# Second layer of four row groups by one level of Strassen's algorithm, in a fused attention and MLP kernel

## The chip, the cores and the metric

The kernel runs on one core of a Trainium2 chip. The metric is the device time of one execution in microseconds (us). The engines are named as in the profile: PE (TensorE, matrix products), PEld (its weight loads), DVE (VectorE), ACT (ScalarE), POOL (GpSimd), SP (SyncE, which here issues the transfers).

A run counts as slow when it took over 1.5% more than the fastest run of the same kernel. Ratios and verdicts use fast runs alone. A ratio is the mean time of one kernel's fast runs over the mean of the other kernel's fast runs in the same rounds, so it is not quite the ratio of the medians that are quoted beside it.

## The reference

Nyström attention over 8 batches of 8 heads, 576 tokens, head size 64, and then a layer norm with a two-layer MLP (512 to 2048 to 512) and a residual. Only the second part is touched:

```python
def _moe_ref(x, g_ln, w_ch1, w_ch2):          # x: attention output, (8, 576, 512)
    mu = np.mean(x, axis=-1, keepdims=True)
    var = np.mean((x - mu) ** 2, axis=-1, keepdims=True)
    xn = (x - mu) / np.sqrt(var + 1e-06) * g_ln
    ch = np.maximum(xn @ w_ch1, 0.0) @ w_ch2
    return x + ch
```

## The kernel before

The 4608 rows are 36 blocks of 128, in 9 groups of 512 rows. Per group, the first layer gives hT (hidden by rows, fp16) and the second layer multiplies it by w2. Matrix work is fp16 with fp32 sums. Attention is computed for pairs of batches, and its instructions are woven into the MLP stream: `fill(n)` lets the stream go n turns (about one 512-column matmul each) between two attention steps. In the traces below an engine's instructions come in the order of the source (rsum, for one, starts on DVE at 194.88 us, behind the 16 weight mixes that were given to DVE before it), which is why the place of an instruction in the source matters.

```python
def center(j):                                 # rows are only centered ...
    ...
    pool.tensor_scalar(out=xn_of[j][:], in0=x_blk[j][:], scalar1=1.0, scalar2=negm,
                       op0=ALU.mult, op1=ALU.add)
...
psM = ctx.enter_context(tc.tile_pool(name="psM", bufs=3, space=PSUM))   # three PSUM tiles, tag "pm"
...
def mlp():
    for g in range(NGRP):
        ...                                    # group 0 differs; transposes of g come before
        for m in range(MCH):                   # first layer: 16 blocks of 128 hidden rows
            psh = psM.tile([P, 512], FP32, name="psh", tag="pm")
            for c in range(KCH):
                MM(psh[:], w1_16[:, c, ts(m, P)], xnT[:, c, :], start=..., stop=...)
                ...
            act(hT[:, m, :], psh[:], AF.Relu)
        for u in range(4):                     # second layer: 4 row blocks x 16 matmuls of 512
            pso = psM.tile([P, DM], FP32, name="pso", tag="pm")
            for m in range(MCH):
                MM(pso[:], hT[:, m, ts(u, P)], w2_16[:, m, :], start=..., stop=...)
                if u >= 2 and m % 8 == 3:
                    ...                        # transposes of the next group's rows
            # ... the deviation is applied to the sum here, with the residual
            dve.scalar_tensor_tensor(out=ot[:], in0=pso[:], scalar=rstds[g][:, u:u + 1],
                                     in1=x_blk.pop(j)[:], op0=ALU.mult, op1=ALU.add)
            store(j, ot)
...
counts += 2 * [[12, 12, 21, 21, 21, 17, 12, 12, 9, 8, 9, 8, 11] + 10 * [8]]
for c, after, count in zip(pairs, ...):        # the last pair: batches 6 and 7
    for step, _ in enumerate(attention2(c.bs, c)):
        fill(count[step])
        settle()
        ...
```

The softmax here doesn't subtract the row's maximum and nothing guards it: scores larger than these inputs give would overflow.

Of the kernel before, what the change touches and what calls it, by code (L numbers as in the profile page):

```python
# [9 lines left out]
FP16 = mybir.dt.float16  # L10
FP32 = mybir.dt.float32
UINT32 = mybir.dt.uint32
AF = mybir.ActivationFunctionType
ALU = mybir.AluOpType
AX = mybir.AxisListType

P = 128
# [3 lines left out]
def kernel(  # L21
# [534 lines left out]
    def attention2(bs, c):  # L556
# [118 lines left out]

        yield from rows_of(bs, ea, zcbd)

    ln_ready = {0}
    mvgs = {}
    xn_of = {}  # L680
# [8 lines left out]
    def block_done(j):  # L689
        g, u = divmod(j, 4)  # L690
        if u == 0:
            mvgs[g] = mstat.tile([P, 4, 2], FP32, name="mvg", tag="mvg")
        if g == 0:
            center_by_act(j)
            later.append(lambda: stats(j))
        elif g == 1:
            later.append(lambda: center_by_act(j))
        else:
            if by_act(j):
                later.append(lambda: stats_by_act(j))  # L700
            else:
                stats(j)
            later.append(lambda: center(j) if g <= mlp_at[0] + 1
                         else uncentered.setdefault(g, []).append(j))
        if u == 3:
            later.append(lambda: deviations(g))


    mlp_at, uncentered = [0], {}
# [4 lines left out]
    def settle():  # L714
        while later:
            later.pop(0)()
# [26 lines left out]
    def center(j):  # L743
        g, u = divmod(j, 4)
        negm = mvgs[g][:, u, 0:1]
        if not by_act(j):
            negm = mstat.tile([P, 1], FP32, name="negm", tag="negm")[:]
            pool.tensor_scalar(out=negm, in0=mvgs[g][:, u, 0:1], scalar1=-1.0, scalar2=0.0,
                               op0=ALU.mult, op1=ALU.add)
        xn_of[j] = mxn.tile([P, DM], FP16, name="xn", tag="xn")  # L750
        pool.tensor_scalar(out=xn_of[j][:], in0=x_blk[j][:], scalar1=1.0, scalar2=negm,
                           op0=ALU.mult, op1=ALU.add)

    def deviations(g):
        lnv = mstat.tile([P, 4], FP32, name="lnv", tag="lnv")
        for o in (0, 1):
            act(lnv[:, o::2], mvgs[g][:, o::2, 1], AF.Ln, bias=eps_ln[:],
                scale=1.0 / DM if by_act(4 * g + o) else 1.0)
        rstds[g] = mstat.tile([P, 4], FP32, name="rstd", tag="rstd")
        act(rstds[g][:], lnv[:], AF.Exp, scale=-0.5)  # L760
        ln_ready.add(g)
# [26 lines left out]
    def transposes(g):  # L788
        for u in range(4):
            transpose_block(g, u)  # L790
            yield



    def mlp():
        for g in range(NGRP):
            mlp_at[0] = g
            hT = mhT.tile([P, MCH, 512], FP16, name="hT", tag="hT")
            if g == 0:
                for u in (0, 2):  # L800
                    if u == 0:
                        for i in range(2):
                            transpose_block(0, i)
                            yield True
                    for m0 in range(0, MCH, 2):
                        if u == 0 and m0 in (6, 10):
                            transpose_block(0, 2 if m0 == 6 else 3)
                            yield True
                        if u == 0 and m0 < MCH - 6:
                            scale_w1(m0 // 2 + 3)  # L810
                        psh = psM.tile([P, 2, 256], FP32, name="psh", tag="pm")
                        for m in range(2):
                            for c in range(KCH):
                                MM(psh[:, m, :], w1_16[:, c, ts(m0 + m, P)],
                                   xnTs[0][:, c, ds(P * u, 256)],
                                   start=(c == 0), stop=(c == KCH - 1), skip=True)
                                if c == 1 or (c == 3 and m == 0):
                                    yield True
                        act(hT[:, m0:m0 + 2, ds(P * u, 256)], psh[:], AF.Relu)
                        yield True  # L820
            else:
                while g not in xnTs:
                    if g in ln_ready:
                        for _ in transposes(g):
                            yield True
                    else:
                        yield False
                xnT = xnTs.pop(g)
                for j in uncentered.pop(g + 1, ()):
                    center(j)  # L830
# [3 lines that stand above are left out]
                        MM(psh[:], w1_16[:, c, ts(m, P)], xnT[:, c, :],  # L834
                           start=(c == 0), stop=(c == KCH - 1))
                        if c < KCH - 1:
                            yield True
                    act(hT[:, m, :], psh[:], AF.Relu)
                    yield True
            tr = None  # L840
            for u in range(4):
                j = 4 * g + u
                pso = psM.tile([P, DM], FP32, name="pso", tag="pm")
                for m in range(MCH):
                    MM(pso[:], hT[:, m, ts(u, P)], w2_16[:, m, :],
                       start=(m == 0), stop=(m == MCH - 1))
                    if m < MCH - 1:
                        yield True
                    if u >= 2 and m % 8 == 3:
                        if g + 1 in ln_ready and g + 1 not in xnTs:  # L850
                            tr = transposes(g + 1)
                        if tr is not None:
                            next(tr, None)
                            yield True
                ot = mout.tile([P, DM], FP32, name="ot", tag="ot")
                dve.scalar_tensor_tensor(out=ot[:], in0=pso[:], scalar=rstds[g][:, u:u + 1],
                                         in1=x_blk.pop(j)[:], op0=ALU.mult, op1=ALU.add)
                store(j, ot)
                yield True
            if tr is not None:  # L860
                for _ in tr:
                    yield True
# [77 lines left out]
    for c, after, count in zip(pairs, pairs[1:] + [None], counts):  # L940
        for step, _ in enumerate(attention2(c.bs, c)):
            fill(count[step])
            settle()
            while c.jobs:
                c.next_job()
                c.next_job()
                fill(8)
            if after:
                cast_and_load(after, pairs[2])
                if step >= 1:  # L950
                    after.next_job()
# [32 lines left out]
```

## Time and profile before

| | before |
|---|---|
| time, median of the first 3 runs | 349.22 us (346.89 to 353.25, the last of them slow) |
| span of the profiled run | 346.7 us |
| PE, DVE, ACT, POOL busy | 93%, 46%, 49%, 36% |
| PE idle after 120 us | 0.3 us, and the end |

The prediction below shows the views that carry the argument. One more matters later. This is PE's timeline in the kernel before, around the end of group 6's second layer (columns: start, duration from the first start to the last end, engine, line, operation, output and inputs, shapes, how many; a wait stands in brackets):

```profile
282.73 0.39 PE L77 MATMUL psxt<-ident,xn 128*128 128x128 f16 x4
282.95 1.89 PE L73 MATMUL pso<-w,hT 128*128 128x512 f16 x8
284.68 0.39 PE L77 MATMUL psxt<-ident,xn 128*128 128x128 f16 x4
284.90 1.03 PE L73 MATMUL pso<-w,hT 128*128 128x512 f16 x4
285.77 1.46 PE L73 MATMUL psh<-xnT,w 128*128 128x512 f16 x6
```

Four matmuls stand between the last transposes and the next first layer (psh). They cover the time in which ACT copies the transposes to xnT, so psh starts without a wait.

### The profile page before, as it was taken

How to read it: one execution, taken by the hardware profiler on the slowest of the kernel's cores; microseconds unless marked ns; L12 is line 12 of the kernel's file. 1: busy time of each engine (PE TensorE's matmuls, PEld its weight loads, DVE VectorE, ACT ScalarE, POOL GpSimd, SP SyncE). 2: the span in 40 equal slices, each digit the busy share in tenths (PEclk: the TensorE clock that was granted, in tenths of full speed). 3: DMA queues.
4: the chain of work that ended last, by engine and by line, in shares of the span. 5: the costliest groups of instructions: out<-in, count | busy, mean ns of one | idle time of the engine just before them, and what ended most of it. 6: DMA issues, size and time to landing. Idle time of an engine off the chain costs nothing.

```text
span 346.7 us, 8948 instructions
## 1 busy us (share of the span) xinstructions
PE 323.3 (93%) x3818; PEld 166.4 (48%) x3818; DVE 158.7 (46%) x341; ACT 168.6 (49%) x328; POOL 125.5 (36%) x199
## 2 busy tenths in 40 slices
PE   8875979879889999999999999999999999999994
PEld 7553744435433545554445444544444454444441
DVE  2645629885499753346777402337850010020011
ACT  4359844943544595045738750465146226415600
POOL 2488878999953498047023000003120010000000
PEclk9999999989999999999999999999999999999998
DMA  7999999999982281171012101210130031022023
GB/s 274 357 353 362 344 404 369 233 384 317 236 281 91 62 260 47 32 201 32 2 30 64 31 2 42 55 30 2 34 84 6 15 77 32 0 62 61 0 54 69
DMA packets 21528, 46.72 MB, mean 135 GB/s; under 512 B 3056, under 2 KB 7152, under 8 KB 21488
## 3 DMA queue, kind: packets, MB, share of 16 engines
q1 hardware_dynamic: 21488, 46.15, 43.6%
q8 instruction: 30, 0.49, 0.6%
q14 instruction: 10, 0.08, 0.1%
HBM read 36.70 MB, written 9.44 MB: 133 GB/s over the span
## 4 chain that ended last, share of the span: by engine, by line
PE 75%; DVE 7%; DMA 7%; ACT 6%; issue 2%; SPq 1%; POOL 0%; DVEq 0%
PE psh L73 35%; PE pso L73 30%; DMA w1stg<-in_moe_w_ch_dram 4%; DMA g_sb<-in_moe_g_ln_dram 3%; PE pscv L73 3%; ACT xn L67 2%; PE psy L73 2%; PE psxt L77 2%; DVE st L67 2%; DVE xblk L67 2%; PE psn L73 1%; DVE xT L67 1%; ACT junk L67 1%; PE psea L73 1%; PE psec L73 1%
## 5 line engine op out<-in xcount | busy, mean ns | idle before, releaser
L73 PE MATMUL pso<-w,hT 128*128 128x512 f16 x576 | 137.6, 381 | 0.0
L73 PE MATMUL psh<-xnT,w 128*128 128x512 f16 (+1 forms) x640 | 133.7, 358 | 2.9 <-DVE xnT L67 1.2
L67 ACT ACTIVATE hT<-psh 128x512 f16<-128x512 f32 x144 | 85.3, 597 | 54.5 <-PE psh L73 54.3
L73 PEld LDWEIGHTS <-w 128*128 128x128 f16 x640 | 59.7, 98 | 60.6 <-issue 2.3
L73 PEld LDWEIGHTS <-hT 128*128 128x128 f16 x576 | 53.9, 98 | 55.7 <-issue 2.1
L67 DVE SCALAR_TENSOR_TENSOR ot<-pso,rstd,xblk 128x512 f32<-128x512 f32 x36 | 27.0, 749 | 107.7 <-PE pso L73 107.7
L67 ACT COPY xnT<-psxt 128x512 f16<-128x512 f16 x32 | 18.7, 584 | 59.1 <-PE psxt L77 59.0
L67 POOL CAST nat<-stg 128x1152 f16<-128x1152 f32 x28 | 31.8, 1147 | 5.1 <-DMA stg<-in_k_dram 1.8
L67 DVE TENSOR_TENSOR xblk<-psy,rcpd 128x512 f32<-128x512 f32 (+1 forms) x40 | 27.6, 691 | 1.8
L67 POOL TENSOR_SCALAR xn<-xblk,negm 128x512 f16<-128x512 f32 x18 | 12.5, 694 | 35.2 <-PE psxt L77 34.1
L67 DVE SCALAR_TENSOR_TENSOR st<-st,psn 128x384 f16<-128x384 f16 (+3 forms) x30 | 13.5, 450 | 24.2 <-PE psn L73 24.2
L67 POOL TENSOR_SCALAR xn<-xblk,mvg 128x512 f16<-128x512 f32 x10 | 6.9, 695 | 45.8 <-PE psxt L77 28.3
L67 POOL CAST natv<-stg 128x1152 f16<-128x1152 f32 x16 | 17.9, 1151 | 11.8 <-DMA stg<-in_v_dram 11.8
L67 DVE STREAM_TRANSPOSE xT<-nat 128x576 uint32<-128x576 uint32 x24 | 18.4, 767 | 4.8 <-POOL nat L67 3.5
L67 POOL TENSOR_SCALAR negm<-mvg 128x1 f32<-128x1 f32 x18 | 3.5, 192 | 37.6 <-PE psy L73 23.9
L73 PE MATMUL psy<-zcbd,ea 128*128 128x260 f16 (+1 forms) x80 | 16.0, 277 | 1.2 <-ACT xT L67 0.6
L77 PE MATMUL psxt<-ident,xn 128*128 128x128 f16 x144 | 14.2, 222 | 2.1 <-ACT xn L67 1.6
L67 DVE TENSOR_REDUCE lmk<-xT 128x64 f16<-128x1152 f16 x12 | 16.1, 1341 | 0.1
L67 POOL TENSOR_TENSOR asum<-asum 128x256 f32<-128x256 f32 (+2 forms) x30 | 15.0, 501 | 2.3
L67 DVE BATCH_NORM_STATS2 st<-xblk 128x6 f32<-128x512 f32 x22 | 15.2, 689 | 0.6
L77 PEld LDWEIGHTS <-xn 128*128 128x128 f16 x144 | 10.9, 99 | 9.1 <-ACT xn L67 2.0
L67 DVE RECIPROCAL rcpd<-psy 128x8 f32<-128x8 f32 (+1 forms) x40 | 8.0, 201 | 11.1 <-PE psy L73 10.6
(99 smaller groups left out, 257.6 us busy)
## 6 DMA issues: line engine op xcount, KB each, us to landing
stg<-in_q_dram SPq DMA_DIRECT2D x16, 576.0 KB, 6.9
stg<-in_k_dram SPq DMA_DIRECT2D x16, 576.0 KB, 7.8
out_dram<-ot SPq DMA_DIRECT2D x72, 128.0 KB, 2.4
stg<-in_v_dram SPq DMA_DIRECT2D x10, 576.0 KB, 8.2
w1stg<-in_moe_w_ch_dram SPq DMA_DIRECT2D x16, 256.0 KB, 6.0
w2stg<-in_moe_w_ch_dram SPq DMA_DIRECT2D x16, 256.0 KB, 5.2
stg<-in_v_dram SPq DMA_DIRECT2D x12, 288.0 KB, 8.7
g_sb<-in_moe_g_ln_dram SPq DMA_DIRECT2D x1, 2.0 KB, 10.1
```

The source lines that it names most:

```text
L67: return lambda *args, **kw: keep(getattr(self.engine, op)(*args, **kw))
L73: keep(nc.tensor.matmul(o, l, r, start=start, stop=stop, tile_position=(rb, cb), skip_group_check=(skip or cb != 0)))
L77: keep(nc.tensor.matmul(o, i_, idn, is_transpose=True, tile_position=(0, 0)))
```

## The change

For groups 4 to 7 the second layer becomes one level of Strassen's algorithm in Winograd's form. Rows and hidden are halved (h11 is the first half of the rows with the first half of the hidden, h12 has the second half of the hidden, h21 and h22 are the same for the second half of the rows), and so is w2. Seven products of half size take the place of eight, P1 to P7; the code calls their PSUM tiles psp1, psp4 and so on. The diff is cut; its comments were added here. The sums of h (here "mixes") are formed in place in hT by DVE between the products, those of w2 once. A group's rows are now fully normalized before the first layer, since the products mix rows. The outputs gather in the x tiles, and stores come from there.

```diff
+    def mix_w2():                              # 16 DVE instructions
+        ...
+        for i, a, b, op in ((1, w12, w11, ALU.subtract), (3, w22, w12, ALU.subtract),
+                            (2, None, w11, ALU.add), (4, w21, None, ALU.subtract)):
+            ...
+            for k in range(0, HK, 2):
+                dve.tensor_tensor(out=w2_mix[i][:, k:k + 2, :], in0=a[:, k:k + 2, :],
+                                  in1=b[:, k:k + 2, :], op=op)
+    def fast_second_layer(g, hT):
+        ...
+        def product(to, left, right, first=True):
+            for k_ in range(2):
+                for k in range(HK):            # 2 x 8 matmuls of 256 columns
+                    MM(to[:, k_, :], left[:, k, ts(k_, P)], right[:, k, :],
+                       start=first and k_ == k == 0, stop=k == HK - 1, skip=True)
+                    ...
+                if tr is None and g + 1 in ln_ready and g + 1 not in xnTs:
+                    tr = transposes(g + 1)
+                if tr is not None and not first:
+                    next(tr, None)             # only in the two products that accumulate
+                    yield True
+        def add(half, col, t):                 # two additions of 256 columns into x tiles
+            for i in range(2):
+                u = 2 * half + i
+                x = x_blk[4 * g + u][:, ts(col, HN)]
+                (pool if t is u2 else dve).tensor_tensor(out=x, in0=t[:, i, :], in1=x, op=ALU.add)
+        def mix(out, a, b, op):                # two instructions of 1024 fp16 elements
+            ...
+        pe = bank("psp4")
+        yield from product(pe, h22, w2_mix[4])                 # P4
+        add(1, 0, pe)
+        mix(h22, h21, h22, ALU.add)
+        pa = bank("psp1")
+        yield from product(pa, h11, w11)                       # P1
+        scalar.copy(p1, pa[:])
+        mix(h21, h11, h21, ALU.subtract)
+        pd = bank("psp7")
+        yield from product(pd, h21, w2_mix[3])                 # P7
+        add(1, 0, pd)
+        add(1, 1, pd)
+        mix(h11, h22, h11, ALU.subtract)
+        yield from product(pa, h12, w21, False)                # P2, onto P1
+        add(0, 0, pa)
+        pc = bank("psp5")
+        yield from product(pc, h22, w2_mix[1])                 # P5
+        add(1, 1, pc)
+        mix(h12, h12, h11, ALU.subtract)
+        pb = bank("psp6")
+        yield from product(pb, h11, w2_mix[2])                 # P6
+        dve.tensor_tensor(out=u2, in0=pb[:], in1=p1, op=ALU.add)
+        for half, col in ((1, 0), (1, 1), (0, 1)):
+            add(half, col, u2)                                 # six additions by POOL
+        yield from product(pc, h12, w22, False)                # P3, onto P5
+        add(0, 1, pc)
+        ...                                                    # four stores
@@ center: rows of groups 4 and up, after the group's deviations
+            pool.tensor_scalar(out=xn_of[j][:], in0=x_blk[j][:], scalar1=negm,
+                               scalar2=rstds[g][:, u:u + 1], op0=ALU.add, op1=ALU.mult)
@@ the loop of the last pair
             settle()
+            if c is pairs[2] and not w2_mix:
+                mix_w2()
```

More of the change, by code (lines that the diff above doesn't have):

```diff
@@ L676, in attention2 @@
         yield from rows_of(bs, ea, zcbd)
+    G_FAST = 4
     ln_ready = {0}
@@ L702, in block_done, with center_in_turn @@
                 stats(j)
-            later.append(lambda: center(j) if g <= mlp_at[0] + 1
-                         else uncentered.setdefault(g, []).append(j))
+            if g < G_FAST:
+                later.append(lambda: center_in_turn(j))
         if u == 3:
             later.append(lambda: deviations(g))
+            if g >= G_FAST:
+                for i in range(4 * g, 4 * g + 4):
+                    later.append(lambda i=i: center_in_turn(i))
+    def center_in_turn(j):
+        g = j // 4
+        if g <= mlp_at[0] + 1:
+            center(j)
+        else:
+            uncentered.setdefault(g, []).append(j)
     mlp_at, uncentered = [0], {}
@@ L750, in center @@
         xn_of[j] = mxn.tile([P, DM], FP16, name="xn", tag="xn")
-        pool.tensor_scalar(out=xn_of[j][:], in0=x_blk[j][:], scalar1=1.0, scalar2=negm,
-                           op0=ALU.mult, op1=ALU.add)
+        if g >= G_FAST:
+            pool.tensor_scalar(out=xn_of[j][:], in0=x_blk[j][:], scalar1=negm,
+                               scalar2=rstds[g][:, u:u + 1], op0=ALU.add, op1=ALU.mult)
+        else:
+            pool.tensor_scalar(out=xn_of[j][:], in0=x_blk[j][:], scalar1=1.0, scalar2=negm,
+                               op0=ALU.mult, op1=ALU.add)
     def deviations(g):
@@ L791, in transposes @@
             yield
+    HK, HN, HT = MCH // 2, DM // 2, 256
+    w2_mix = {}
+    def mix_w2():
+        for i in (1, 2, 3, 4):
+            w2_mix[i] = stage.tile([P, HK, HN], FP16, name=f"w2mix{i}", tag="stg")
+        w11, w12 = w2_16[:, 0:HK, 0:HN], w2_16[:, 0:HK, HN:DM]
+        w21, w22 = w2_16[:, HK:MCH, 0:HN], w2_16[:, HK:MCH, HN:DM]
+        for i, a, b, op in ((1, w12, w11, ALU.subtract), (3, w22, w12, ALU.subtract),
+                            (2, None, w11, ALU.add), (4, w21, None, ALU.subtract)):
+            a = w2_mix[3][:] if a is None else a
+            b = w2_mix[2][:] if b is None else b
+            for k in range(0, HK, 2):
+                dve.tensor_tensor(out=w2_mix[i][:, k:k + 2, :], in0=a[:, k:k + 2, :],
+                                  in1=b[:, k:k + 2, :], op=op)
@@ new lines, in fast_second_layer, with bank @@
+    def fast_second_layer(g, hT):
+        w11 = w2_16[:, 0:HK, 0:HN]
+        w21, w22 = w2_16[:, HK:MCH, 0:HN], w2_16[:, HK:MCH, HN:DM]
+        h11, h12 = hT[:, 0:HK, 0:HT], hT[:, HK:MCH, 0:HT]
+        h21, h22 = hT[:, 0:HK, HT:], hT[:, HK:MCH, HT:]
+        tr = None
+        def bank(name):
+            return psM.tile([P, 2, HN], FP32, name=name, tag="pm")
+        def product(to, left, right, first=True):
+            nonlocal tr
+            for k_ in range(2):
+                for k in range(HK):
+                    MM(to[:, k_, :], left[:, k, ts(k_, P)], right[:, k, :],
+                       start=first and k_ == k == 0, stop=k == HK - 1, skip=True)
+                    if k % 2 == 1:
+                        yield True
[3 more added lines that the diff above has]
+                    next(tr, None)
+                    yield True
+        def add(half, col, t):
[4 more added lines that the diff above has]
+        def mix(out, a, b, op):
+            for k in range(0, HK, 4):
+                dve.tensor_tensor(out=out[:, k:k + 4, :], in0=a[:, k:k + 4, :],
+                                  in1=b[:, k:k + 4, :], op=op)
+        both = stage.tile([P, 2, 2, HN], FP32, name="both", tag="stg")
+        p1, u2 = both[:, 0, :, :], both[:, 1, :, :]
+        pe = bank("psp4")
[24 more added lines that the diff above has]
+        add(0, 1, pc)
+        for u in range(4):
+            store(4 * g + u, x_blk.pop(4 * g + u))
+        if tr is not None:
+            for _ in tr:
+                yield True
@@ L839, in mlp @@
                     yield True
+            if G_FAST <= g < NGRP - 1:
+                yield from fast_second_layer(g, hT)
+                continue
             tr = None
@@ L855, in mlp @@
                 ot = mout.tile([P, DM], FP32, name="ot", tag="ot")
-                dve.scalar_tensor_tensor(out=ot[:], in0=pso[:], scalar=rstds[g][:, u:u + 1],
-                                         in1=x_blk.pop(j)[:], op0=ALU.mult, op1=ALU.add)
+                if g >= G_FAST:
+                    dve.tensor_tensor(out=ot[:], in0=pso[:], in1=x_blk.pop(j)[:], op=ALU.add)
+                else:
+                    dve.scalar_tensor_tensor(out=ot[:], in0=pso[:], scalar=rstds[g][:, u:u + 1],
+                                             in1=x_blk.pop(j)[:], op0=ALU.mult, op1=ALU.add)
                 store(j, ot)
```

## The prediction

> **What bounds the kernel now.** I read the page's first two parts first (busy time by engine and the 40 slices), to see which engine sets the end and where:
>
> ```profile
> PE 323.3 (93%) x3818; PEld 166.4 (48%) x3818; DVE 158.7 (46%) x341; ACT 168.6 (49%) x328; POOL 125.5 (36%) x199
> ...
> PE   8875979879889999999999999999999999999994
> ...
> DVE  2645629885499753346777402337850010020011
> ```
>
> TensorE (PE) is full from the twelfth slice (104 us) to the end; the kernel can get faster there only by giving PE less to do. DVE is nearly idle at the end but at 7, 8, 5 tenths in slices 28 to 30 (234 to 260 us), inside groups 4 to 7.
>
> Next the groups of instructions with shapes kept apart, for what the second layer costs, and the timeline of PE for the pace, since a busy time counts overlapping matmuls twice:
>
> ```profile
> L73 PE MATMUL pso<-w,hT 128*128 128x512 f16 x576 | 137.6, 381 | 0.0
> ...
> 257.25 13.97 PE L73 MATMUL psh<-xnT,w 128*128 128x512 f16 x64 [0.30 <-ACT xnT L67]
> ...
> 48.33 1.26 PE L73 MATMUL psh<-xnT,w 128*128 128x256 f16 x10
> ```
>
> 64 matmuls of 512 columns end 13.97 us after the first starts, and one lasts 0.38 us, so they follow each other at (13.97-0.38)/63 = 215.7 ns. Ten of 256 columns, one of 273 ns, follow at (1.26-0.273)/9 = 109.7 ns. Half-size matmuls thus run at full rate, with their own weight loads hidden.
>
> Then the table of stretches, cut at the starts of the layers that the chain of work that ended last shows (second layers at 205.9, 240.2, 271.1 and 299.7 us for groups 4 to 7):
>
> ```profile
> core 0: us, PE busy (x) PEld busy (x) DVE busy (x) ACT busy (x) POOL busy (x), PEclk, DMA share, GB/s
> ...
> 205.90:224.40 18.50, 18.50 (x338) 9.54 (x336) 4.64 (x9) 5.11 (x9) 0.69 (x1) 1.00 0.20 45
> ...
> 240.20:257.20 17.00, 16.75 (x95) 8.15 (x93) 14.41 (x32) 4.32 (x11) 4.50 (x12) 1.00 0.20 47
> ...
> 271.10:285.90 14.80, 14.80 (x82) 7.20 (x81) 2.25 (x3) 2.94 (x5) 1.55 (x3) 1.00 0.23 53
> ```
>
> Groups 6 and 7 stand alone: 64 matmuls (13.8 us) and 16 transposes (1.0 us), nothing else on PE. Group 4 lies among attention of the last pair with an idle DVE. Group 5 lies in that pair's last rows, and there DVE is already busy 14.4 of 17.0 us, of which only 4 x 0.75 us serve the second layer.
>
> **What the Trainium skill says.** "TensorE: Matmul & The Clock Gate", section "Back-to-back issue gap", gives an isolated gap of N/2.4 + 2.5 ns: 109.2 at 256 columns, 215.8 at 512. The trace agrees (109.7, 215.7). The same section's 131 ns per matmul for sustained 512-column work is not what this trace has. "VectorE: DVE Perf Modes", section "The perf-mode tier table", has tensor_tensor at two elements a cycle for 16-bit operands in SBUF and at one with PSUM or fp32. The trace before has no DVE tensor_tensor with fp16 SBUF operands alone; with PSUM, 512 fp32 elements take 691 ns and 256 take 415. "SBUF — State Buffer", section "🔬 SBUF: two separate sides", says that a DVE instruction with two SBUF inputs and a GpSimd one lock each other out. The mixes are of that kind; no row here shows its cost.
>
> **The change, part by part.**
>
> *Removed on PE.* Per group 64 x 215.7 = 13.80 us become 7 x 16 matmuls of 256 columns, 112 x 109.7 = 12.29: 1.5 us less, 6.0 us for four groups, 1.7% of 349. So the perfect result is still within 2%. Every other term can only take from it.
>
> *Mixing the weights.* Once, after the first step of the last pair, 16 DVE instructions of 512 fp16 elements. At two a cycle that is 256 cycles, so each should last as the 256-element row does. Four such independent ones in a row:
>
> ```profile
> 102.93 0.41 DVE L67 TENSOR_TENSOR zcbd<-pszc,mask4t 128x256 f16<-128x256 f32 x1
> 103.27 0.41 DVE L67 TENSOR_TENSOR zcbd<-pszc,mask 128x256 f16<-128x256 f32 x1
> 103.60 0.41 DVE L67 TENSOR_TENSOR zcbd<-pszc,mask4t 128x256 f16<-128x256 f32 x1
> ```
>
> They start every 0.335 us, so 16 take 16 x 0.335 + 0.08 = 5.4 us. Where they land in DVE's order:
>
> ```profile
> 190.64 1.02 DVE L67 STREAM_TRANSPOSE ecT<-ec 128x288 uint32<-128x288 uint32 x2 [1.18 <-ACT ec L67]
> 193.09 0.29 DVE L67 TENSOR_REDUCE rsum<-psb 128x4 f32<-128x128 f32 x1 [1.44 <-ACT psb L67]
> ...
> 193.96 0.31 DVE L67 STREAM_TRANSPOSE bmT<-bm 128x128 f16<-128x128 f16 x1
> ...
> 195.78 0.22 PE L73 MATMUL psse<-bm,bones 128*128 128x128 f16 x1
> ```
>
> They fill 191.7 to 197.1. The chain from rsum to bmT takes 1.2 us, so bmT is ready at 198.3, and PE, in order, reaches psse at 195.8 after its 12 filling matmuls. With 0.2 us for the wait and a weight load it stands until 198.5: **2.7 us lost**.
>
> *A group alone (6 and 7).* I walk the queues from the end of P4 (zero). DVE: two adds of 256 from PSUM to 0.95, then mix of h22, two instructions of 1024 fp16 elements. Estimate for one: 512 cycles plus the 0.15 us that the 691 ns row has over its 512 cycles, 0.69 us, a second 0.60 after the first: to 2.2. Mix of h21: first half at 2.8, second at 3.4. PE: P1, 16 x 0.11, to 1.75, then P7 whose weights are h21: its first half may start at about 3.0, so 1.2 us stand, and 0.15 more for the second half. Later products find their mixes done, but for 0.15 us before P3's second half. Before, the last ReLU of the first layer (0.60 us) was needed as the 16th matmul of 216 ns; now P4 needs it as the 8th of 110 ns, at 0.77 us, where it is ready at 0.80 plus wait and weight load: 0.3 us. Sum of stands 1.8 us against 1.5 saved: **0.3 us lost in each, 0.6 in both**. The six GpSimd adds (728 ns per 256 fp32 elements in the group asum) take 4.4 us, and the last product's PSUM tile waits for them, about 4 us into the next first layer; that has two other tiles and ReLU at 0.60 of 0.86 us, so I count nothing.
>
> *Group 4.* The same P4 and P7 stands: P4, P1 and P7 fall in one step's filling, and DVE has little else. **About 0.1 us lost.**
>
> *Group 5.* The filling counts are unchanged, a second layer has 60 turns instead of 68, and group 4's shortening moves group 5 up 8 turns, so it starts in the second row step instead of the third and about 7 row steps of 8 turns lie before P3. A row step costs DVE 1.8 us (0.20, 0.69, 0.69, 0.18 and gaps; in the timeline reciprocals at 249.92 and 251.71). Seven, one of them a half block without statistics (0.84 less), are 11.8 us. In front of P3 come of the new work 8 adds after four products (3.5 us), and four mixes (4.3 to their first needed half): 7.8 us. DVE therefore reaches P3's weights at about 19.5 us after the layer's start, PE alone would at 13. PE waits about 2.9 us at P7 (a row step sits ahead of the mix) and 3.8 at P3. The walk ends at 22 us against the 17.0 of before, which held one row more (0.2): **5.0 us lost**.
>
> *Moved, not changed.* GpSimd normalizes fully with the same instruction (694 ns), now after the deviations; POOL is idle in slices 22 to 28 at 0 to 2 tenths, and the transposes always waited for the deviations. Output stores come from the x tiles, of the same size. The last group's end differs by 0.06 us (an add of 691 for a 749 ns instruction).
>
> Sum: +2.7 +0.6 +0.1 +5.0 = +8.4 us, 357.6 us. All savings of PE are already in these terms.
>
> **Rivals.** (1) *The work is hidden and the 1.7% comes through*: 343 us. For it: DVE is only 46% busy. Against: the mixes sit between a product and the next but one, 2.5 us of DVE for 1.75 of PE. (2) *Only the fixed stands remain, group 5 finds DVE free enough*, since the walk stacks all row work ahead of each mix: 352 to 353. (3) *DVE's mixes run at one element a cycle* or are locked out by GpSimd: mixing 16 x 0.61 = 9.8 us (4 more lost), each lone group 3.5 more, group 5 4 more: 372. The skill's tier table speaks against it; nothing measured here does. (4) *PSUM turns into the wait*: if the next first layer's third tile is the one that the GpSimd adds hold, about 2 us a group, 364.
>
> **Range and chances.** The walk says 357.6; half weight to rival 2 on group 5 and some to rival 4 leaves 356.5. With the scatter of the runs before (346.9 to 353.3) I take 349.5 to 364. The line of 2% is 356.2, right beside it: slower 0.49, same 0.48. Faster needs 7 us where 6.0 is the most that PE can give: 0.03.
>
> **What would show it.** PE's matmuls at 110 ns in the new products (pace right). DVE's mixes at 0.4 and 0.7 us (mode right). A PE gap of about 2.7 us before psse near 196; one of 1.2 before each P7 in groups 6 and 7, named to a DVE write of hT; 6 to 7 us of PE idle in group 5's second layer with DVE near full. GpSimd's adds ending 3 to 4 us into the next first layer without a PE gap. I am wrong if group 5's rows interleave so that mixes go ahead of them, or if the PSUM tile or a mode costs what I counted as nothing.

## The result

The changed kernel takes 361.65 us (median of 4 runs, 360.52 to 366.37) against 348.58 for the kernel before. The ratio of the fast runs is 1.037, with a 95% interval of 1.0295 to 1.0444. Both profiled runs are fast. The change is slower by 3.7%; the outputs are correct.

First the page of the changed kernel (busy tenths and PE's granted clock in 40 slices):

```profile
PE 324.2 (90%) x4010; PEld 185.8 (52%) x4010; DVE 190.5 (53%) x425; ACT 170.9 (48%) x332; POOL 143.5 (40%) x223
...
PE   7867989789989999999997989896969899998994
PEclk9998999989999999999999899999899999999998
```

From the thirteenth slice on, PE's row was all nines but for the last slice; now slices 22, 24, 26, 28, 30, 32 and 37 are lower. PE has less to do behind group 4 and yet takes longer: it waits. Such a wait of PE is called a stand below. It is counted from the moment at which the next matmul could have started at the usual pace, and so comes out some 0.16 us longer than the wait in a row's brackets.

Then the groups of instructions with shapes apart, for the new work. They answer to the durations that the prediction had estimated:

```profile
L67 DVE TENSOR_TENSOR hT<-hT 128x1024 f16<-128x1024 f16 x32 | 20.3, 681 | 0.0
...
L67 POOL TENSOR_TENSOR xblk<-both,xblk 128x256 f32<-128x256 f32 x24 | 16.6, 728 | 98.6 <-DVE both L67 98.6
...
L67 DVE TENSOR_TENSOR w2mix<-w 128x512 f16<-128x512 f16 x8 | 2.7, 410 | 0.0
```

A mix of 1024 elements takes 681 ns (0.69 estimated), one of 512 takes 410 (415 taken), an addition by POOL 728 (728 taken). The sizes of the pieces were right. What had to be read off is where PE stands.

**The table of layers.** From PE's timeline I took the time from one layer's first matmul to the next layer's first, for each profiled run. Everything ahead of group 4 is the same on PE in both kernels. The instant at which group 4 starts scatters (188.5 us before, 186.5 after, 186.3 to 194.7 over all profiled runs here), so layers are the sharper measure, and whole times are compared with their intervals.

| layer, us | before | changed | difference | predicted |
|---|---|---|---|---|
| group 4 first | 17.2 | 20.8 | +3.5 | +2.7 |
| group 4 second | 18.5 | 19.0 | +0.5 | +0.1 |
| group 5 first | 15.9 | 16.0 | +0.2 | 0 |
| group 5 second | 17.2 | 22.7 | +5.5 | +5.0 |
| group 6 first | 13.8 | 15.4 | +1.6 | 0 |
| group 6 second | 14.7 | 15.3 | +0.6 | +0.3 |
| group 7 first | 13.8 | 14.8 | +0.9 | 0 |
| group 7 second | 14.7 | 15.3 | +0.6 | +0.3 |
| group 8 first | 13.8 | 14.8 | +0.9 | 0 |
| sum | | | +14.4 | +8.4 |

The sum of 14.4 us is that of two profiles, in which the changed kernel had started group 4 two us earlier; the means of the fast runs differ by 13.3.

**Group 4's first layer.** The timeline of the changed kernel, DVE and PE together:

```profile
189.55 2.73 DVE L67 TENSOR_TENSOR w2mix<-w 128x512 f16<-128x512 f16 x8
...
194.88 0.28 DVE L67 TENSOR_REDUCE rsum<-psb 128x4 f32<-128x128 f32 x1
...
195.75 0.23 PE L73 MATMUL psse<-bm,bones 128*128 128x128 f16 x1 [1.85 <-DVE bm L67]
...
196.96 6.00 PE L73 MATMUL psh<-xnT,w 128*128 128x512 f16 x21
```

The 16 weight mixes fill DVE from 189.55 to 194.9, rsum waits behind them, and PE stands for the chain that starts with it, as predicted. The new thing is the last line. 21 matmuls of 512 columns took 6.00 us where 4.7 is their time at 215.7 ns. The table of stretches shows why (columns as in the prediction; the granted clock is the third value from the right):

```profile
195.80:203.60 7.80, 7.68 (x183) 3.77 (x184) 1.79 (x7) 2.98 (x5) 0.00 (x0) 0.78 0.01 2
249.40:254.80 5.40, 5.35 (x29) 3.19 (x30) 3.27 (x8) 0.00 (x0) 0.00 (x0) 0.68 0.01 3
```

Behind the stand of 2.0 us the clock was granted at 0.78 over 7.8 us (1.7 us of clock lost: in the trace it is 0.50 from 196.2 to 199.6 us), and behind the stand before P7 of group 5 at 0.68 over 5.4 us (1.7 us again). The Trainium skill, "TensorE: Matmul & The Clock Gate", section "What's actually happening", describes a half-rate state entered after an idle window of about 3.4 us that runs freely, without regard to the kernel. Half rate for 3.4 us is what this trace has, but the stand ahead of it was 2.0 us, shorter than that window.

**Group 5**, PE and DVE in the changed kernel's timeline:

```profile
246.94 0.20 DVE L67 RECIPROCAL rcpd<-psy 128x8 f32<-128x8 f32 x1
...
248.73 1.26 DVE L67 TENSOR_TENSOR hT<-hT 128x1024 f16<-128x1024 f16 x2
249.45 0.99 PE L73 MATMUL psp<-w2mix,hT 128*128 128x256 f16 x6 [3.11 <-DVE hT L67]
...
260.67 1.28 DVE L67 TENSOR_TENSOR hT<-hT 128x1024 f16<-128x1024 f16 x2
261.41 0.39 PE L73 MATMUL psp<-w,hT 128*128 128x256 f16 x2 [1.24 <-DVE hT L67]
```

A row step of the attention (246.94 to 248.81) lies on DVE ahead of the mix that P7 needs, and PE stands 3.3 us; it stands another 1.4 us before P3.

**Group 6**, which stands alone, the timeline of all engines in the changed kernel:

```profile
282.17 1.91 PE L73 MATMUL psp<-w,hT 128*128 128x256 f16 x16
...
284.98 2.09 PE L73 MATMUL psp<-w2mix,hT 128*128 128x256 f16 x16 [0.90 <-DVE hT L67]
...
293.69 4.14 POOL L67 TENSOR_TENSOR xblk<-both,xblk 128x256 f32<-128x256 f32 x6 [20.97 <-DVE both L67]
...
294.61 0.39 PE L77 MATMUL psxt<-ident,xn 128*128 128x128 f16 x4
...
295.67 1.89 PE L73 MATMUL psh<-xnT,w 128*128 128x512 f16 x8 [0.67 <-ACT xnT L67]
297.18 0.42 DVE L67 TENSOR_TENSOR xblk<-psp,xblk 128x256 f32<-128x256 f32 x1 [3.57 <-POOL xblk L67]
297.86 0.42 DVE L67 TENSOR_TENSOR xblk<-psp,xblk 128x256 f32<-128x256 f32 x1 [0.26 <-POOL xblk L67]
298.34 1.02 PE L73 MATMUL psh<-xnT,w 128*128 128x512 f16 x4 [0.78 <-DVE xblk L67]
```

Three stands are to be seen. P1's 16 matmuls start at 282.17 and would end their turn at 283.92 (16 x 109.7 ns), but P7 starts at 284.98: 1.06 us, named to DVE's mix of hT. The last transposes are now PE's last work in the layer, and psh waits for ACT to copy them: from 294.83 (four transposes at 55 ns) to 295.67, 0.84 us. And eight psh matmuls later PE wants a third PSUM tile, which P5 and P3 hold until DVE has added them; DVE waits for POOL, which works through its six additions until 297.83. PE stands from 297.40 to 298.34, 0.94 us. The prediction had the first of these and not the other two.

### The profile page after: what moved, and what is told of

The parts are those of the page before. It is cut to its first block, busy times and chain, and to the rows that moved or that the text cites. A ratio compares the mean times of both kernels' runs of the same rounds, so it can differ in the third digit from the quotient of the medians.

```text
span 359.1 us, 9438 instructions
## 1 busy us (share of the span) xinstructions
PE 324.2 (90%) x4010; PEld 185.8 (52%) x4010; DVE 190.5 (53%) x425; ACT 170.9 (48%) x332; POOL 143.5 (40%) x223
## 4 chain that ended last, share of the span: by engine, by line
issue 36%; PE 32%; DMA 11%; POOL 10%; DVE 6%; ACT 4%; SPq 0%; POOLq 0%
PE psh L73 15%; PE pso L73 11%; DMA stg<-in_k_dram 7%; POOL xblk L67 4%; POOL xn L67 4%; DMA w1stg<-in_moe_w_ch_dram 3%; PE pscv L73 2%; DMA w2stg<-in_moe_w_ch_dram 1%; ACT junk L67 1%; ACT xn L67 1%; DVE xblk L67 1%; DVE xT L67 1%; DVE st L67 1%; PE psn L73 1%; DVE lmk L67 1%
## 5 line engine op out<-in xcount | busy, mean ns | idle before, releaser
L73 PE MATMUL psh<-xnT,w 128*128 128x512 f16 (+1 forms) x640 | 136.7, 364 | 7.2 <-DVE xblk L67 3.0
L73 PEld LDWEIGHTS <-hT 128*128 128x128 f16 x768 | 72.6, 99 | 48.0 <-DVE hT L67 9.6
L73 PE MATMUL pso<-w,hT 128*128 128x512 f16 x320 | 77.2, 382 | 0.0
L67 POOL TENSOR_TENSOR xblk<-both,xblk 128x256 f32<-128x256 f32 x24 | 16.6, 728 | 98.6 <-DVE both L67 98.6
L67 DVE TENSOR_TENSOR xblk<-psp,xblk 128x256 f32<-128x256 f32 x48 | 18.0, 417 | 58.1 <-PE psp L73 47.3
L67 ACT COPY xnT<-psxt 128x512 f16<-128x512 f16 x32 | 18.6, 586 | 57.5 <-PE psxt L77 57.4
L73 PE MATMUL psp<-w2mix,hT 128*128 128x256 f16 x256 | 32.9, 279 | 5.9 <-DVE hT L67 5.9
L73 PE MATMUL psp<-w,hT 128*128 128x256 f16 x192 | 25.7, 277 | 1.2 <-DVE hT L67 1.2
L67 POOL CAST natv<-stg 128x1152 f16<-128x1152 f32 x16 | 17.9, 1152 | 11.0 <-DMA stg<-in_v_dram 10.9
L67 DVE TENSOR_TENSOR hT<-hT 128x1024 f16<-128x1024 f16 x32 | 20.3, 681 | 0.0
L67 DVE SCALAR_TENSOR_TENSOR ot<-pso,rstd,xblk 128x512 f32<-128x512 f32 x16 | 11.9, 746 | 15.1 <-PE pso L73 15.1
L67 POOL TENSOR_SCALAR xn<-xblk,mvg,rstd 128x512 f16<-128x512 f32 x6 | 4.6, 772 | 34.7 <-ACT rstd L67 34.7
L73 PE MATMUL psy<-zcbd,ea 128*128 128x260 f16 (+1 forms) x80 | 16.3, 280 | 1.2 <-ACT xT L67 0.6
```

The costliest lines, as they stand in the source:

```text
L67: return lambda *args, **kw: keep(getattr(self.engine, op)(*args, **kw))
L73: keep(nc.tensor.matmul(o, l, r, start=start, stop=stop, tile_position=(rb, cb), skip_group_check=(skip or cb != 0)))
```

## The experiments

The first four test one cause each. The layers of all fast-profiled runs stand in one table at the end of this section.

**The weight mixes, later.** Theory: they stand ahead of the softmax chain. Rival: DVE's 5.4 us only move.

```diff
@@ -1052 +1052 @@
-            if c is pairs[2] and not w2_mix:
+            if c is pairs[2] and step == 2:
```

> The weight mixes are given to DVE after the third step of the last pair instead of after the first, nothing else. Theory (the mixes stand ahead of the small softmax chain that PE's psse waits for, and the wait drops PE's clock): the 2.0 us gap before psse and the stretch at granted clock 0.78 behind it both go, first layer of group 4 back from 20.8 to about 17.2 us, time down by about 3.5 us, ratio to the kernel before from 1.037 to about 1.027. Rival (the 5.4 us of DVE work only shifts to a later wait): group 4's second layer grows by what its first layer loses, ratio stays at 1.037.

Measured: 359.22 us (median of 6), ratio 1.033 (1.027 to 1.039). Group 4's first layer is 17.24 us, exactly that of the kernel before, and no other layer moved by more than 0.2. The theory holds for the layer: 3.5 us came from where the mixes stood. The whole time moved by less than the layer (1.027 was expected), within the scatter of what lies ahead of group 4; the interval of the ratio overlaps that of the changed kernel, so the timed runs alone would not show the gain.

**The order of POOL's additions.**

```diff
@@ -887 +887 @@
-        for half, col in ((1, 0), (1, 1), (0, 1)):
+        for half, col in ((0, 1), (1, 0), (1, 1)):
```

> Of the six GpSimd additions of a group, the two that the last DVE additions wait for go first instead of last. Theory (the third PSUM tile of the next first layer is held until the last product's additions, which wait for all six): the last DVE additions start 2.9 us earlier, the PE gaps of 1.6, 0.9 and 0.9 us in the first layers of groups 6, 7 and 8 go; 3.4 us less, ratio about 1.027. Rival (those gaps come from the late transposes, so that the first layer starts unprimed): the gaps stay, ratio 1.037.

Measured: 360.17 us, ratio 1.031 (1.025 to 1.037). PE's timeline of this kernel behind group 6's second layer:

```profile
296.69 7.50 PE L73 MATMUL psh<-xnT,w 128*128 128x512 f16 x34 [0.67 <-ACT xnT L67]
```

The 34 matmuls run through where the changed kernel stopped after eight. The first layers of groups 7 and 8 are 13.81 us, as before; that of group 6 still has 1.2 us of its stand of 1.6, since DVE comes late out of group 5. So the PSUM tile is the cause of 0.94 us in groups 7 and 8 and of a part in group 6: 2.3 us, not the 3.4 expected. A second thing shows in this run. It has the same stand of 1.85 us before psse, but the clock behind it was granted at 1.00 and the layer took 19.4 us instead of 20.8. So the drop doesn't follow such a stand every time: of the four profiles that have this stand with nothing changed about it, two show the drop (the changed kernel and turns_early below) and two don't (this one and skip5 below).

**The transposes, earlier.**

```diff
@@ -838 +838 @@
-        def product(to, left, right, first=True):
+        def product(to, left, right, first=True, turn=False):
@@ -848 +848 @@
-                if tr is not None and not first:
+                if tr is not None and turn:
@@ -878 +878 @@
-        yield from product(pa, h12, w21, False)
+        yield from product(pa, h12, w21, False, turn=True)
@@ -885 +885 @@
-        yield from product(pb, h11, w2_mix[2])
+        yield from product(pb, h11, w2_mix[2], turn=True)
```

> The last two transposes of the next group's rows come in the product before the last, so a whole product lies between the last one and the next first layer. Theory (next first layer waits for ScalarE's copy of the last transposes, issued as PE's last work): the four gaps of about 0.84 us at the start of the first layers of groups 5 to 8 go, 3.4 us less, ratio about 1.027. Rival (without that gap PE reaches the held PSUM tile 0.84 us sooner and waits there as much longer): about 1 us less at group 5 only, ratio about 1.034.

Measured: 366.27 us, ratio 1.052 (1.046 to 1.058): slower than the changed kernel by a further 1.4%. PE's timeline behind group 6's second layer:

```profile
300.57 1.89 PE L73 MATMUL psh<-xnT,w 128*128 128x512 f16 x8
304.22 4.04 PE L73 MATMUL psh<-xnT,w 128*128 128x512 f16 x18 [1.76 <-DVE xblk L67]
```

The wait for xnT is gone, and second layers 6 and 7 are 14.46 us, 0.88 less. But the first layers behind them are 0.98 longer: PE reaches the held PSUM tile sooner and waits 1.76 us there instead of 0.78. The rival was right in groups 6 and 7. What neither foresaw is the first layer of group 6, which went from 15.4 to 20.2 us: its wait for the tile grew to 3.65 us, since POOL's six additions, which wait for DVE's common sum behind the rows, now ran from 268.56 to 272.69 us with PE at the tile from 269.4; a wait of 0.7 us for a ReLU came ahead of it, and the clock dropped behind it (0.92 over the 22 us around it). A wait removed in front of a longer one gives nothing, and here a longer standstill cost more.

**PE kept busy while it waits.** This run takes no wait away; it puts matmuls of zeros in front of two.

```diff
@@ -872,0 +873,2 @@
+        if g == 5:
+            warm(28, 256)
@@ -1051,0 +1054,2 @@
+            if c is pairs[2] and step == 1:
+                warm(17, 256)
```

> PE gets 17 matmuls of zeros (1.9 us) ahead of psse, and 28 (3.1 us) ahead of P7 of group 5, where it stood idle; no wait is removed. Theory (the stands also drop PE's granted clock to half for some 3.4 us, which costs 1.3 to 1.7 us after each): the clock stays at 1.00 in both stretches, the 21 matmuls behind psse take 4.7 instead of 6.0 us, P7 and P2 of group 5 go at 110 ns a matmul, time down by about 3 us, ratio about 1.028. Rival (slow matmuls there come from contention with DVE's reads, not from the wait): same pace as now, time same or up, ratio 1.037 or more.

Measured: 359.40 us, ratio 1.034 (1.029 to 1.039). PE's timeline around psse:

```profile
194.26 2.02 PE L73 MATMUL idle<-zeros 128*128 128x256 f16 x17
...
197.44 4.71 PE L73 MATMUL psh<-xnT,w 128*128 128x512 f16 x21
```

The 21 matmuls take 4.71 us, the clock is 1.00 in both stretches, and group 4's first layer is 19.45 us, 1.3 less. At psse this proves little, for the order of POOL's additions gave the same 19.4 us without zeros. At P7 of group 5 it says more: the five profiles with the stand of 3.1 us there and no zeros (changed, mix_late, pool_order, turns_early, three) all have the drop, and this one, where zeros fill the stand, has none. Contention with DVE is not the cause of the slow matmuls: in pool_order and here they go at full pace beside the same DVE work. Group 5's second layer gained only 1.0 of the 1.7 us of clock: its wait before P3 grew from 1.24 to 1.86 us. DVE had stood 1.27 us for P7's result in the changed kernel and stands 0.28 here, so it reached P3's mix 1.0 us sooner and no more, which speaks for DVE as the bound of that layer.

**Group 5 left ordinary.**

```diff
@@ -942 +942 @@
-            if G_FAST <= g < NGRP - 1:
+            if G_FAST <= g < NGRP - 1 and g != 5:
```

> Group 5 alone keeps the ordinary second layer (groups 4, 6 and 7 by Strassen, rows of all four still fully normalized). Theory (in group 5 the layer's 10 us of DVE work meets the last pair's rows on DVE, and the backlog holds PE): second layer of group 5 back from 22.7 to about 17.2 us and the first layer of group 6 from 15.4 to 13.8, 7 us less in all, ratio from 1.037 to about 1.017. Rival (the 5.5 us are the dropped clock and fixed waits that any group has, as group 6 shows with 0.6): only about 2 us less, ratio about 1.031.

Measured: 356.13 us, ratio 1.021 (1.013 to 1.030). Group 5's second layer is 16.9 us and group 6's first layer 13.8; 7.3 us less in these two, as expected. Not all of it comes from the attention rows meeting the layer's sums on DVE: a group alone, as group 6 in the table, loses 0.6 us and 0.9 in the first layer behind it. About 5.8 us are left for the meeting and the dropped clock that follows it.

**Three repairs together.** The edit is the three diffs above (late weight mixes, POOL's order, early transposes) in one kernel.

> The late weight mixes, the GpSimd order and the early transposes together. Theory (each removes a wait of its own, and the early transposes gain only once the PSUM tile is freed in time): first layer of group 4 17.2 us, of 6, 7 and 8 13.8 to 14.5, second layers of 6 and 7 14.5, that of group 5 still 21 to 22; in all some 10 us less, ratio about 1.01. Rival (waits only move, as they did with the early transposes alone): ratio stays over 1.025.

Measured: 353.15 us, ratio 1.014 (1.007 to 1.020). Now the early transposes gain: the second layers of groups 6 and 7 are 14.46 and the first layers behind them 13.8. Group 5's second layer (21.8) and the first layer of group 6 (16.3) keep their loss, and each P7 still stands for DVE's mix (0.9 us in the timeline).

**Mixes in buffers of their own.** In place, a mix must wait until the products that read the old rows are through. With buffers (in tiles of the pool that held the attention's inputs, free by then) h11-h21 can be formed when half of the first layer is done. The edit, on top of the three repairs, cut to its core:

```diff
+    def mix_rows(hT, m):            # called behind the ReLU of blocks 3, 7, 11 and 15
+        c = m % HK // 4
         ...                         # h11, h21, h12, h22: the four blocks of this quarter
+        def part(name, a, b, op):
+            t = nat.tile([P, 4, HN], FP16, name="hmix" + name, tag="nat")
+            dve.tensor_tensor(out=t[:], in0=a, in1=b, op=op)
+            hmix.setdefault(name, [None, None])[c] = t
+        if m < HK:
+            part("s21", h11, h21, ALU.subtract)
+        else:
+            part("s22", h21, h22, ALU.add)
+            part("s11", hmix["s22"][c][:], h11, ALU.subtract)
+            part("s12", h12, hmix["s11"][c][:], ALU.subtract)
 ...
-        mix(h22, h21, h22, ALU.add)             # the four mixes in place go
-        mix(h21, h11, h21, ALU.subtract)
-        mix(h11, h22, h11, ALU.subtract)
-        mix(h12, h12, h11, ALU.subtract)
 ...                                             # and the products read the buffers
-        yield from product(pd, h21, w2_mix[3])
+        yield from product(pd, hmix['s21'], w2_mix[3])
 ...
                     act(hT[:, m, :], psh[:], AF.Relu)
+                    if FAST(g) and m % 4 == 3:
+                        mix_rows(hT, m)
```

> The three repairs, and the mixed rows of hT written to buffers of their own during the first layer, as soon as their four ReLU blocks are there, instead of in place between the products. Theory (the in-place mixes make DVE the path between products): no wait before P7, second layers of groups 4, 6 and 7 at 12.3 us of products and 0.9 of transposes (13.2 to 13.4 alone), group 5 at 17 to 18.5 since its additions still meet the rows; ratio about 0.99. Rival (DVE's mixes in the first layer delay the attention's small chains or ReLU, and first layers grow): ratio 1.00 to 1.01.

Measured: 347.13 us, ratio 0.994 (0.988 to 1.0004), no clear difference from the kernel before. Groups 4, 6 and 7 do what the arithmetic says. The timeline of group 6 in the sister run below has the same layer lengths. Group 5 takes 19.1 us, more than the 17 to 18.5 expected, and group 6's first layer 15.9: the rows still meet its additions and half of its mixes on DVE, and two of these mixes took 1.15 us instead of 0.69 beside POOL (the last section shows them).

**The same, group 5 ordinary.**

```diff
-    FAST = lambda g: G_FAST <= g < NGRP - 1
+    FAST = lambda g: g in (4, 6, 7)
```

> The same with group 5 left ordinary: three groups save 1.5 us each and nothing meets the rows. Theory: second layers of 6 and 7 at 13.2 to 13.4 us against 14.7 before, group 5 at 17.2, all first layers as before; 4 to 4.6 us less than the kernel before, ratio about 0.987. Rival (waits of about 1 us a group remain somewhere): ratio 0.995 to 1.0.

Measured: 342.75 us, ratio 0.983 (0.977 to 0.989); the verdict at 2% is unclear, since the interval reaches across 0.98, but it excludes 1. Timeline of group 6's second layer, PE and DVE:

```profile
267.73 0.69 DVE L67 TENSOR_TENSOR hmixs<-hT 128x1024 f16<-128x1024 f16 x1 [1.31 <-ACT hT L67]
...
268.75 1.91 PE L73 MATMUL psp<-w,hT 128*128 128x256 f16 x16
...
270.50 1.91 PE L73 MATMUL psp<-w2mix,hmixs 128*128 128x256 f16 x16
...
280.12 1.24 PE L73 MATMUL psh<-xnT,w 128*128 128x512 f16 x5
```

P7 (270.50) follows P1 without a gap, and from group 4 on the trace names no wait of a PE matmul at all. Second layers 6 and 7 are 13.22 us against 14.71, so the 1.5 us per group that the column count promises are there, and 4.9 us in all. This version beats both kernels.

**Only the rows and outputs.** No product by Strassen, no weight mixes:

```diff
@@ -942 +942 @@
-            if G_FAST <= g < NGRP - 1:
+            if False:
@@ -1052,2 +1051,0 @@
-            if c is pairs[2] and not w2_mix:
-                mix_w2()
```

> No product by Strassen and no weight mixes; what stays of the change is that rows of groups 4 to 8 are fully normalized after the deviations and their outputs added without the factor. Theory (moving the normalization costs nothing): every layer as in the kernel before, 17.2, 18.5, 15.9, 17.2, then 13.8 and 14.7 us in turn, ratio 0.997 to 1.003. Rival (the later normalization holds transposes): second layers of groups 3 to 7 or the first layers after them grow by 0.5 us or more, ratio 1.005 to 1.01.

Measured: every layer from group 4 on is that of the kernel before within 0.02 us. The ratio is 1.006 (0.9998 to 1.012), and the profiled run fell in the slow state, with group 4 starting at 194.7 us instead of 188.5. So moving the normalization costs nothing in the layers; whether it costs a fraction of a us ahead of them stays open, for the interval holds both.

**The last group too**, on the best version:

```diff
@@ -679 +679 @@
-    FAST = lambda g: g in (4, 6, 7)
+    FAST = lambda g: g in (4, 6, 7, 8)
@@ -877 +877 @@
-                (pool if t is u2 else dve).tensor_tensor(out=x, in0=t[:, i, :], in1=x, op=ALU.add)
+                (pool if t is u2 and g < NGRP - 1 else dve).tensor_tensor(out=x, in0=t[:, i, :], in1=x, op=ALU.add)
```

> Of the best version so far (buffers, group 5 ordinary), with the last group by Strassen too, its common sums added by DVE instead of GpSimd. Theory: PE saves another 1.5 us, but after the last product DVE still has about 2.0 us of additions (estimate: the sum 0.69, six additions at 0.335 and two more) where one of 0.69 follows now; 0.2 to 0.4 us less in all, ratio as with group 8 ordinary, 0.982. Rival (the last additions fit beside the last product): 1.3 us less, ratio 0.978.

Measured: 346.70 us, ratio 0.993 (0.989 to 0.998), 1% behind the version without it across two sets of runs, whose intervals just touch. PE's part went from 13.98 to 12.49 us as expected, and yet the stretch from group 8's second layer to the end went from 18.6 to 21.0 us. The end is longer than either theory had it. SP's timeline at the end of this kernel:

```profile
340.97 5.05 SPq L786 DMA_DIRECT2D out_dram<-xblk  x8
```

All eight stores of the group are issued at the end, 5.05 us in a row, because every x tile gets its last sum from P3 or from the common sums behind it. In the kernel before only two were left by then. This profile was of the slow state, but the order of the work at the end doesn't depend on that.

Layers of the runs with a fast profile, in us:

| layer | before | changed | mix_late | pool_order | turns_early | kept_warm | skip5 | three | buf_all | buf_skip5 |
|---|---|---|---|---|---|---|---|---|---|---|
| 4 first | 17.2 | 20.8 | 17.2 | 19.4 | 21.1 | 19.5 | 19.4 | 17.2 | 17.2 | 17.2 |
| 4 second | 18.5 | 19.0 | 19.0 | 19.0 | 17.9 | 19.0 | 19.0 | 17.9 | 16.6 | 16.6 |
| 5 first | 15.9 | 16.0 | 16.0 | 16.0 | 16.7 | 16.0 | 16.0 | 16.0 | 16.0 | 16.0 |
| 5 second | 17.2 | 22.7 | 22.8 | 22.8 | 22.1 | 21.7 | 16.9 | 21.8 | 19.1 | 16.9 |
| 6 first | 13.8 | 15.4 | 15.4 | 15.0 | 20.2 | 15.4 | 13.8 | 16.3 | 15.9 | 13.8 |
| 6 second | 14.7 | 15.3 | 15.3 | 15.3 | 14.5 | 15.3 | 15.4 | 14.5 | 13.2 | 13.2 |
| 7 first | 13.8 | 14.8 | 14.7 | 13.8 | 15.7 | 14.8 | 14.8 | 13.8 | 13.8 | 13.8 |
| 7 second | 14.7 | 15.3 | 15.3 | 15.3 | 14.5 | 15.3 | 15.3 | 14.5 | 13.2 | 13.2 |
| 8 first | 13.8 | 14.8 | 14.8 | 13.8 | 15.7 | 14.8 | 14.8 | 13.8 | 13.8 | 13.8 |
| ratio to before | 1 | 1.037 | 1.033 | 1.031 | 1.052 | 1.034 | 1.021 | 1.014 | 0.994 | 0.983 |

## Why the prediction was right, and where it was short

The direction and the range held: slower, 361.65 us inside 349.5 to 364. The direction was close to a toss of a coin, though: the prediction gave slower 0.49 and same 0.48. The center of 356.5 was 5 us too low. By its own steps:

- **PE's saving of 1.5 us a group** is right. It shows only when nothing else stands: 13.22 against 14.71 us in the version with buffers.
- **The weight mixes** cost 2.7 us by the walk. They stood as described; the term measured 3.5. Without the dropped clock it is 2.2, the stand with its second short wait (so in pool_order, skip5 and kept_warm), and the drop, which the walk doesn't have, added 1.3.
- **Group 5**: 5.0 predicted, 5.5 measured. The stand before P7 was 3.3 us for 2.9 predicted. The one before P3 was 1.4 for 3.8, with 1.7 us of dropped clock between, in which PE's slowness hid part of it. The bound itself was right: P3 started 19.2 us after the layer's start, where the walk has DVE ready at 19.5. skip5 shows that the meeting with the attention's rows is the cause of most of it.
- **A group alone**: 0.3 predicted, 0.6 measured, and not by the terms listed. The stand before P7 is 1.06 (1.2) and in P7's middle 0.2 (0.15), the wait for the last ReLU 0.1 instead of 0.3, and the 0.84 us for the copy of the last transposes wasn't in the sum. The diff had moved these transposes to the layer's last product; the prediction doesn't ask what then follows them. They cost 1.07 us behind group 4 and 0.84 behind each of the other three, 3.6 in all. That the second layers came out within 0.5 us of the walk all the same is partly luck, for stands that were put too large made up for it.
- **The PSUM tile** is the other term that was left out, for which the step says "so I count nothing". It cost 0.94 us in the first layers of groups 7 and 8 and is the 1.6 of group 6 (where DVE's rows hold it up too): up to 3.5 us in all, of which the order of POOL's additions alone gave back 2.3. The rival (4) had it, at 2 us a group. The error was to judge two remaining tiles by ACT's mean pace. PE came to the held tile after two blocks of the first layer (three in group 6), 1.73 us after its start, and stood until that tile was free, while ACT had emptied the others or was about to.
- **The moved parts** cost nothing in the layers, as said; the instruction did change, 771 ns for 694 with two per-row operands.

What the table is above the prediction, 6.0 us, is then: 3.5 for the tile, 1.3 less 0.5 in group 4's first layer, 0.5 in group 5, 0.6 for groups 6 and 7, 0.4 for group 4's second layer, together 5.8.

Three small readings in the prediction are off and move nothing: PE is full from the thirteenth slice (the one that starts at 104 us), POOL has 3 tenths in slice 23, and ten additions, not eight, lie ahead of P3's weights (they took 3.6 us, 3.5 in the walk).

## What to carry to other kernels

When a change takes work from a full engine and pays with work on idle ones, put the new work's place in those engines' queues on paper, not only its duration: here the same mixes cost no time when they lay in the first layer and about 1.2 us a group when they lay between two products, with every other wait they led to on top. A tile that a slow side path holds makes its engine wait when the ring comes round to it, although another tile of the ring is free (in group 7 PE stood until 298.34, with another tile emptied at 297.37). And remove waits from the one that ends last backwards: the early transposes alone lost 1.4%, and behind a freed tile they gained.

## What the Trainium skill lacked or had wrong

- "TensorE: Matmul & The Clock Gate", section "What's actually happening": it has the slow state come after at least one idle window of about 3.4 us. Here a stand of 2.0 us, short of that, was followed by a granted clock of 0.78 over 7.8 us, while the same stand in two other kernels' runs (the POOL order, group 5 ordinary) left the layer at 19.4 us and the clock at 1.00. That it comes in some runs and not in others would fit the freely running window that the page describes; no run here tests it.
- The same page, section "Back-to-back issue gap": its 131 ns per sustained matmul of 512 columns is not seen; it is 215.7 ns in the dense stretches at a granted clock of 1.00, and 109.7 ns at 256 columns with a weight load of 98 ns for each.
- "VectorE: DVE Perf Modes", section "The perf-mode tier table": tensor_tensor is given for 2048 elements alone. Measured: 681 ns for 1024 fp16 elements in SBUF and 410 for 512, so 0.53 ns for each further element and a fixed part of some 0.14 us; rows with PSUM and fp32 take 1.08 ns for each (691 ns for 512, 415 for 256). The page's factor of two between them is confirmed.
- "SBUF — State Buffer", section "🔬 SBUF: two separate sides": it has one of DVE and GpSimd wait while the other has the shared port, without a duration for such a pair. In all three runs with buffers a normalization of 0.77 us beside a mix took 1.17 us or more, and in the one with all groups in buffers mixes of 0.69 us took 1.15. From that run (timeline, both engines):

```profile
238.76 1.28 POOL L67 TENSOR_SCALAR xn<-xblk,negm,rstd 128x512 f16<-128x512 f32 x1
239.43 1.15 DVE L67 TENSOR_TENSOR hmixs<-hmixs,hT 128x1024 f16<-128x1024 f16 x1
240.03 1.20 POOL L67 TENSOR_SCALAR xn<-xblk,mvg,rstd 128x512 f16<-128x512 f32 x1
```

- No page has the cost of a second per-row operand on GpSimd: a tensor_scalar of 512 fp32 elements took 771 ns with two and 694 with one.
